# Running the fp32 transposes of a retention and mixture-of-adapters kernel as pairs of 64-row array tiles

## The chip, the cores and the metric

The kernel runs on one core of one Trainium2 chip. TensorE (PE) multiplies, and its weight loads are shown as an engine of their own (PEld); VectorE (DVE) and ScalarE (ACT) read what it leaves in PSUM; GpSimd (POOL) works on SBUF alone; SyncE (SP) issues transfers. The metric is the device time of one execution in microseconds (us); lower is better. A difference under 1% can't be told from no change here.

## The reference

```python
# q, k, v: [8 batches, 8 heads, 576 rows, 64]
scores = scale * q @ k.transpose(0, 1, 3, 2)
gamma  = 1.0 - 2.0 ** (-5.0 - arange(H))
ret    = scores * where(rel >= 0, gamma ** rel, 0.0)     # rel = row - column: causal decay
x      = (ret @ v) as [4608 tokens, 512]                 # heads side by side
# mixture of adapters: 8 experts of rank 16, the best 2 of each token
logits = x @ w_gate
w      = softmax over the 2 largest logits
out    = x + sum over those two of w * (x @ A[e]) @ B[e]
```

## The kernel before

The rows are cut into chunks of 128 (four full ones, and a last one of 64). A **unit** is one chunk of a pair of batches: 16 full units (t = 0 to 15, chunk by chunk, four batch pairs in each) and 4 half units (t = 16 to 19). Two units in a row share one load: a **quad**, which is q, k and v of four batches for one chunk. A quad is loaded by one transfer each for q, k and v (the first quad by halves), and up to three quads are in SBUF (`io`, 3 buffers). `issue(n)` names the quad two ahead of the one in work.

For each unit the code writes these stages, and each engine does its own in the order that a scheduling layer made of the code, close to the written one:

- **T** (`stage_T`, L191): q and k, which lie with rows on partitions, are transposed on TensorE (L206) to `pt_q` and `pt_k` in PSUM: 16 transposes of 128x128 fp32 in a full unit, 8 in a half one. DVE multiplies `pt_q` by the decay `aqp` into `qT` (L219), ACT copies `pt_k` into `kT` (L228).
- **S** (`stage_S`, L234): scores of two heads at once, on two 64-row halves of the array (L261), then the causal mask on DVE into `rt` (L272; `rh` in half units, L280).
- **O** (`stage_O`, L293): the carried state `P` times `qT` into `px` (L309; not in the first chunk), and the new state `pu` from k and v (L323), added on DVE (`pn`) and decayed on POOL. v has been scaled before on POOL (`scale_v`, L184).
- **R** (`stage_R`, L345): `rt` times v onto `px` (L358; L376 in half units). ACT copies `px` to `xT`, which is x transposed.
- **Z** (`stage_Z`, L389): x times all A and the gate, into `pz` (L396); then a chain of small operations that picks two experts: DVE `lg`, `m8`, `ns`, ACT `sg` (L417), DVE `cm`, `zc`.
- **X** (`stage_X`, L436): `zc` is transposed (fp16, L442) and copied to `zT` by ACT.
- **Y** (`stage_Y`, L450): `xT` is transposed back into `po` (L457, 4 transposes of 128x128 fp32 for each batch, 8 in a full unit), the adapter output is added there (L466, fp16), ACT copies `po` to `osb`, and SP writes it out.

A full unit is written S(t), O(t), R(t), X(t-1), T(t+1), Y(t-1), Z(t). PSUM has 8 buffers of one bank each (`pp`), which all these tiles share in turn. The constants `pack` (identities, masks, decays), `aqp`, A and the gate are loaded from ACT's queue at the start, beside the first q and k on SP's.

Of the kernel before, what the change touches and what calls it, by code (L numbers as in the profile page):

```python
# [18 lines left out]
def kernel(  # L19
# [10 lines left out]
    nc = tc.nc  # L30
# [17 lines left out]
    swap_np = np.roll(np.eye(128, dtype=np.float32), 64, axis=1)  # L48
# [6 lines left out]
    for hp in range(HP):  # L55
# [25 lines left out]
    swap32 = pack[:, 128:256]
    tri = pack[:, 256:384]
    trih = pack[:, 384:448]
    gv = pack[:, 448 : 448 + H]
    gvh = pack[:, 448 + H : 448 + 2 * H]
    g128 = pack[:, 448 + 2 * H : 448 + 2 * H + HP]
# [52 lines left out]
    aqp = cpool.tile([128, HP, 128], FP32, tag="aqp", name="aqp")  # L139
    nc.scalar.dma_start(out=aqp, in_=dr_aqp.ap())  # L140
    AW = []
    for par in range(2):
        AW.append(cpool.tile([128, HP, ER + E], FP32, tag=f"AW{par}", name=f"AW{par}"))
    for dt in range(HP):
        nc.scalar.dma_start(
            out=AW[0][:, dt, 0:ER].rearrange("p (e r) -> p e r", e=E),
            in_=moe_A[:, 128 * dt : 128 * dt + 128, :].rearrange("e d r -> d e r"),
        )
        nc.scalar.dma_start(
            out=AW[0][:, dt, ER : ER + E],  # L150
            in_=moe_w_gate[128 * dt : 128 * dt + 128, :],
        )
    Bcat = cpool.tile([128, Dm], FP16, tag="Bcat", name="Bcat")
    nc.gpsimd.dma_start(out=Bcat, in_=moe_B.rearrange("e r d -> (e r) d"))
    ident16 = cpool.tile([128, 128], FP16, tag="ident16", name="ident16")
    nc.gpsimd.tensor_copy(out=ident16, in_=ident32)
    for ho in range(2):
        nc.gpsimd.tensor_copy(
            out=AW[1][64 * ho : 64 * ho + 64],
            in_=AW[0][64 - 64 * ho : 128 - 64 * ho],  # L160
        )
    issue(1)

# [8 lines left out]
    ]  # L172

# [17 lines left out]
    def stage_T(t):  # L191
# [5 lines left out]
        nb = 2 if full else 1  # L197
        hpg = 2 if full else 4
        L = 128 if full else LH
        for g in range(HP // hpg):  # L200
            for src, dst, nm in ((q32, qT, "q"), (k32, kT, "k")):
                ps = pp.tile([128, hpg, nb, 128], FP32, tag="pb", name=f"pt_{nm}")
                for a in range(hpg):
                    hp = g * hpg + a
                    for b in range(nb):
# [8 lines left out]
                pv = ps.rearrange("p a b (c i) -> p a (b c) i", i=L)  # L214
                dv = dst.rearrange("p a b i -> p a (b i)")[
                    :, g * hpg : g * hpg + hpg, 0 : 2 * L
                ].rearrange("p a (b i) -> p a b i", i=L)
                if nm == "q":
                    nc.vector.tensor_tensor(  # L219
                        out=dv,  # L220
                        in0=pv,
                        in1=aqp[:, g * hpg : g * hpg + hpg, 0:L]
                        .unsqueeze(2)
                        .broadcast_to((128, hpg, 2, L)),
                        op=ALU.mult,
                    )
                else:
                    nc.scalar.copy(out=dv, in_=pv)  # L228
# [64 lines left out]
    def stage_O(t):  # L293
# [10 lines left out]
        if c > 0:  # L304
# [40 lines left out]
    def stage_R(t):  # L345
# [24 lines left out]
        else:  # L370
            for hp in range(HP):
                for b in range(2):
                    for ho in range(2):
# [6 lines left out]
                            start=False,  # L380
# [3 lines left out]
            xt = mo.tile([128, HP, 128], FP32, tag="xT", name="xT", bufs=6)  # L384
            for b in range(2):
                nc.scalar.copy(out=xt[:, :, LH * b : LH * b + LH], in_=px[b])  # L386
# [62 lines left out]

    def stage_Y(t):  # L450
# [3 lines left out]
        for b in range(len(s["xT"])):  # L454
            po = pp.tile([128, Dm], FP32, tag="pb", name="po")
            for dt in range(HP):
                nc.tensor.matmul(  # L457
                    po[:, 128 * dt : 128 * dt + 128],
                    lhsT=s["xT"][b][:, dt, :],
                    rhs=swap32 if b else ident32,  # L460
                    is_transpose=True,
                    start=(dt == 0),
                    stop=False,
                    skip_group_check=True,
                )
            nc.tensor.matmul(  # L466
                po, lhsT=s["zT"][:, b, :], rhs=Bcat, start=False, stop=True,
                skip_group_check=True,
            )
            osb = mo.tile([128, Dm], FP32, tag="osb", name="osb", bufs=4)  # L470
            nc.scalar.copy(out=osb, in_=po)  # L471
            if full:
                n0 = S * (2 * bp + b) + 128 * c
                nc.sync.dma_start(out=out[n0 : n0 + 128, :], in_=osb)
            else:
                for par in range(2):
                    n0 = S * (2 * bp + par) + 128 * c
# [6 lines left out]
    scale_v(0)  # L484
    for t in range(NU):
# [18 lines left out]
        stage_Z(t)  # L504
# [33 lines left out]
```

## Time and profile before

| | |
|---|---|
| median of 3 runs | 226.03 us (224.5 to 226.05) |
| the profiled execution | 225.21 us |
| its span in the profile | 223.4 us |
| busy: TensorE, its weight loads | 200.8 us (90%), 182.4 us (82%) |
| busy: DVE, ACT, POOL | 105.9 us (47%), 80.6 us (36%), 59.8 us (27%) |
| moved by DMA | 39.11 MB, 175 GB/s over the span |

The profiled execution is 0.4% under the median. What lies outside its span is 1.8 us.

### The profile page before, as it was taken

To read this page: it belongs to the slowest core of one execution; us is meant where nothing else is said; L and a number is where in the kernel's file an instruction comes from. 1 tells how busy PE (TensorE), PEld (TensorE's weight loads), DVE (VectorE), ACT (ScalarE), POOL (GpSimd) and SP (SyncE) were. 2 spreads that over 40 slices of the span, in tenths; PEclk is the share of its full clock that TensorE was granted. 3 is DMA by queue.
4 is the path that set the end of the run, shared out by engine and by line. 5 is a ranking of instruction groups with operands and counts; after the bars stand their busy time and mean duration, and the time that the engine had idled before them with its cause. 6 is when DMAs were issued, how large, how long until landed. Compare 5 with 4: busy or idle time off the path is not lost.

```text
span 223.4 us, 7090 instructions
## 1 busy us (share of the span) xinstructions
PE 200.8 (90%) x3096; PEld 182.4 (82%) x3096; DVE 105.9 (47%) x272; ACT 80.6 (36%) x170; POOL 59.8 (27%) x61
## 2 busy tenths in 40 slices
PE   0197979899999899999999999999999999999951
PEld 0186969698999799999999989999999999978840
DVE  0115552827273927272727292727272727244430
ACT  0041525051513260616161506161615151544431
POOL 3016320711812520902530622090501321000000
PEclk9999999999999999999999999999999999999995
DMA  7999998999699999999999798967555520222212
GB/s 167 182 201 220 189 230 185 218 221 234 141 230 271 211 204 237 271 201 213 303 222 191 227 203 194 220 191 183 139 130 147 140 89 7 98 97 50 50 47 47
DMA packets 57342, 39.11 MB, mean 175 GB/s; under 512 B 30816, under 2 KB 52576, under 8 KB 57312
## 3 DMA queue, kind: packets, MB, share of 16 engines
q1 hardware_dynamic: 52144, 37.75, 75.0%
q10 hardware_dynamic: 5024, 0.78, 2.7%
q8 instruction: 24, 0.39, 0.8%
q0 software_dynamic: 144, 0.13, 0.4%
q14 instruction: 6, 0.05, 0.1%
HBM read 29.35 MB, written 9.44 MB: 174 GB/s over the span
## 4 chain that ended last, share of the span: by engine, by line
PE 73%; DMA 9%; DVE 8%; SPq 5%; ACT 1%; issue 1%; ACTq 1%
PE pz L396 14%; PE px L358 11%; PE ps_s L261 10%; PE po L457 7%; PE px L309 6%; PE pt_k L206 6%; PE pt_q L206 6%; DMA k<-in_k_dram 6%; PE pu L323 5%; SPq L98 5%; PE po L466 4%; DMA AW<-in_moe_A_dram 3%; DVE rt L272 3%; DVE cm L422 2%; PE pzt L442 2%
## 5 line engine op out<-in xcount | busy, mean ns | idle before, releaser
L219 DVE TENSOR_TENSOR qT<-pt_q,aqp 128x512 f32<-128x512 f32 x36 | 24.9, 692 | 48.9 <-PE pt_q L206 48.9
L184 POOL TENSOR_TENSOR v<-v,pack 128x512 f32<-128x512 f32 x36 | 36.6, 1042 | 35.1 <-DMA v<-in_v_dram 34.8
L367 ACT COPY xT<-px 128x512 f32<-128x512 f32 x32 | 18.8, 587 | 69.6 <-PE px L358 69.6
L338 POOL TENSOR_TENSOR P<-pn,gdec 128x512 f32<-128x512 f32 x16 | 20.4, 1276 | 81.4 <-DVE pn L337 62.3
L272 DVE TENSOR_TENSOR rt<-ps_s,pack 128x512 f32<-128x512 f32 x64 | 39.6, 682 | 2.2 <-PE ps_s L261 2.2
L396 PE MATMUL pz<-AW,xT 128*128 128x136 f32 x288 | 36.7, 279 | 0.7 <-ACT xT L386 0.7
L396 PEld LDWEIGHTS pz<-AW,xT 128*128 128x128 f32 x288 | 35.9, 190 | 1.4 <-ACT xT L386 0.9
L261 PE MATMUL ps_s<-qT,kT 64*128 64x128 f32 (+1 forms) x640 | 36.7, 272 | 0.0
L261 PEld LDWEIGHTS ps_s<-qT,kT 64*128 64x128 f32 (+1 forms) x640 | 33.1, 181 | 2.8 <-issue 0.3
L358 PE MATMUL px<-rt,v 128*64 128x128 f32 x512 | 34.4, 275 | 0.8 <-DVE rt L272 0.7
L358 PEld LDWEIGHTS px<-rt,v 128*64 128x64 f32 x512 | 29.1, 137 | 3.0 <-DVE rt L272 2.5
L206 PE MATMUL pt_q<-pack,q 128*128 128x128 f32 x144 | 22.9, 283 | 7.2 <-DMA q<-in_q_dram 7.2
L409 DVE COPY lg<-pz 128x16 f32<-128x16 f32 (+1 forms) x20 | 3.5, 173 | 50.1 <-PE pz L396 50.1
L206 PE MATMUL pt_k<-pack,k 128*128 128x128 f32 x144 | 22.6, 281 | 4.4 <-DMA k<-in_k_dram 4.4
L228 ACT COPY kT<-pt_k 128x512 f32<-128x512 f32 x36 | 21.2, 588 | 12.0 <-PE pt_k L206 12.0
L471 ACT COPY osb<-po 128x512 f32<-128x512 f32 x36 | 21.0, 586 | 5.1 <-PE po L466 2.8
L206 PEld LDWEIGHTS pt_q<-pack,q 128*128 128x128 f32 x144 | 16.6, 145 | 7.5 <-issue 7.3
L417 ACT ACTIVATE sg<-lg,ns 128x8 f32<-128x8 f32 x36 | 9.1, 294 | 36.1 <-DVE ns L412 36.1
L457 PE MATMUL po<-pack,xT 128*128 128x128 f32 x144 | 21.9, 274 | 0.0
L206 PEld LDWEIGHTS pt_k<-pack,k 128*128 128x128 f32 x144 | 17.5, 145 | 5.0 <-DMA k<-in_k_dram 3.7
L323 PE MATMUL pu<-v,k 128*64 128x64 f32 x512 | 18.9, 225 | 1.7 <-POOL v L184 1.7
L323 PEld LDWEIGHTS pu<-v,k 128*64 128x64 f32 x512 | 16.4, 138 | 4.7 <-POOL v L184 2.3
(28 smaller groups left out, 137.5 us busy)
## 6 DMA issues: line engine op xcount, KB each, us to landing
out_dram<-osb SPq DMA_DIRECT2D x32, 256.0 KB, 3.7
q<-in_q_dram SPq DMA_DIRECT2D x2, 512.0 KB, 7.2
k<-in_k_dram SPq DMA_DIRECT2D x2, 512.0 KB, 9.0
v<-in_v_dram SPq DMA_DIRECT2D x2, 512.0 KB, 7.1
q<-in_q_dram SPq DMA_DIRECT2D x8, 128.0 KB, 3.8
k<-in_k_dram SPq DMA_DIRECT2D x8, 128.0 KB, 3.2
v<-in_v_dram SPq DMA_DIRECT2D x8, 128.0 KB, 3.5
out_dram<-osb SPq DMA_DIRECT2D x8, 128.0 KB, 2.3
```

Source lines behind the costliest of these rows:

```text
L184: nc.gpsimd.tensor_tensor(out=v32[:, b * H : b * H + H, :], in0=v32[:, b * H : b * H + H, :], in1=g.unsqueeze(2).broadcast_to((128, H, Dh) ...
L206: nc.tensor.matmul(ps[:, a, b, :], lhsT=src[:, b * H + 2 * hp : b * H + 2 * hp + 2, :], rhs=ident32, is_transpose=True, start=True, stop=True,
L219: nc.vector.tensor_tensor(out=dv, in0=pv, in1=aqp[:, g * hpg : g * hpg + hpg, 0:L] .unsqueeze(2) .broadcast_to((128, hpg, 2, L)), op=ALU.mult,
L228: nc.scalar.copy(out=dv, in_=pv)
L261: nc.tensor.matmul(o, lhsT=kT[sl, hp, b, :], rhs=qT[sl, hp, b, :], start=(a == 0 and (b == 0 or not full)), stop=True, skip_group_check=True,)
L272: nc.vector.tensor_tensor(out=r.rearrange("p a b i -> p (a b) i"), in0=ps[ho].rearrange("p a b i -> p (a b) i"), in1=tri.unsqueeze(1).broa ...
L323: nc.tensor.matmul(pu[64 * ho : 64 * ho + 64, hp, b, :], lhsT=s["k"][:, b * H + h, :], rhs=s["v"][:, b * H + h, :], start=(hp == 0 and b = ...
L338: nc.gpsimd.tensor_tensor(out=pf, in0=pn, in1=gdec.rearrange("p a b d -> p (a b d)"), op=ALU.mult,)
L358: nc.tensor.matmul(px[b][64 * cc : 64 * cc + 64, hp, :], lhsT=s["v"][:, b * H + h, :], rhs=rt[h][:, b, :], start=(c == 0 and hp == 0), sto ...
L396: nc.tensor.matmul(pz[:, b, :], lhsT=xts[b][:, dt, :], rhs=AW[b][:, dt, :], start=(dt == 0), stop=(dt == HP - 1), skip_group_check=True,)
L457: nc.tensor.matmul(po[:, 128 * dt : 128 * dt + 128], lhsT=s["xT"][b][:, dt, :], rhs=swap32 if b else ident32, is_transpose=True, start=(dt ...
L471: nc.scalar.copy(out=osb, in_=po)
```

## The change

Every 128x128 fp32 transpose becomes two products: rows 0 to 63 and rows 64 to 127 of the source are each loaded as weights (64 rows, 128 columns) and meet a 64x64 identity (`id64`), so that each gives 64 output columns. The two go to two PSUM banks. `stage_T` makes two tiles for q and two for k, by row half and no longer by head pair; the fp32 transposes of Y stand in a stage of their own, `stage_B`; `stage_Y` keeps the fp16 products, now four of 256 columns in place of two of 512, and four copies of 256 elements in place of two of 512. A unit is now written S(t), O(t), R(t), T(t+1), B(t-1), X(t-1), Z(t), Y(t-1), for half units too. In half units the state's product goes to a bank of its own (`pq`), ACT copies it, and DVE adds `px` to it in place of ACT's copy. `osb` has 3 buffers for both batches in place of 4 for one. Constants are split and go through SP's queue: `id64` first, `aqp` behind the first q, `pack` behind the first k, A and the gate behind the first v. A `Sigmoid` on one element at the start makes ACT load its table there.

```diff
+    id64 = cpool.tile([128, 64], FP32, tag="id64", name="id64")
+    nc.sync.dma_start(out=id64, in_=dr_first.ap())
+    warm = cpool.tile([128, 1], FP32, tag="warm", name="warm")
+    nc.scalar.activation(out=warm, in_=warm, func=AFT.Sigmoid)
...
+                if split and lo == 0 and src is k:
+                    nc.sync.dma_start(out=aqp, in_=dr_aqp.ap())
+                if split and lo == 0 and src is v:
+                    nc.sync.dma_start(out=pack, in_=dr_rest.ap())
+                if split and lo == 2 and src is q:
+                    load_moe()
...
-                        nc.tensor.matmul(
-                            ps[:, a, b, :],
-                            lhsT=src[:, b * H + 2 * hp : b * H + 2 * hp + 2, :],
-                            rhs=ident32,
...
+            for hp in range(HP):
+                for b in range(2 if full else 1):
+                    for r in range(2):
+                        sl = slice(64 * r, 64 * r + 64)
                         nc.tensor.matmul(
+                            ps[r][:, hp, b, :] if full else ps[r][:, hp, :],
+                            lhsT=src[sl, b * H + 2 * hp : b * H + 2 * hp + 2, :],
+                            rhs=id64[sl, :],
                             is_transpose=True,
...
-            for b in range(2):
-                nc.scalar.copy(out=xt[:, :, LH * b : LH * b + LH], in_=px[b])
+            xt = s["xh"]
+            for b in range(2):
+                xs = xt[:, :, LH * b : LH * b + LH]
+                nc.vector.tensor_tensor(out=xs, in0=px[b], in1=xs, op=ALU.add)
...
+    def stage_B(t):
...
+        for b in range(n):
+            for dt in range(HP):
+                for cc in range(2):
+                    sl = slice(64 * cc, 64 * cc + 64)
+                    nc.tensor.matmul(
+                        po[cc][:, b, dt, :],
+                        lhsT=s["xT"][b][sl, dt, :],
+                        rhs=id64[sl, :],
+                        is_transpose=True,
...
     def stage_Y(t):
...
+        for cc in range(2):
+            for b in range(n):
                 nc.tensor.matmul(
+                    po[cc][:, b, :, :],
+                    lhsT=s["zT"][:, b, :],
+                    rhs=bv[:, :, cc ^ b, :],
...
+        for cc in range(2):
+            for b in range(n):
+                nc.scalar.copy(out=osb[:, b, :, cc ^ b, :], in_=po[cc][:, b])
...
-        full = units[t][0] < NFULL
-        if full:
-            stage_R(t)
-        if t > 0:
-            stage_X(t - 1)
-        if not full:
-            stage_Y(t - 1)
-            stage_R(t)
+        stage_R(t)
         if t + 1 < NU:
             stage_T(t + 1)
-        if full and t > 0:
+        if t > 0:
+            stage_B(t - 1)
+            stage_X(t - 1)
+        stage_Z(t)
+        if t > 0:
             stage_Y(t - 1)
-        stage_Z(t)
```

On TensorE, from the end of R to the next unit's scores, a full unit reads so before (a number behind a name is that of a buffer; weight loads of fp32 products are not listed apart):

```order
L442 MATMUL pzt<-ident_95,zc 128x128
L206 MATMUL pt_q<-pack,q_712 128x128 x4
L206 MATMUL pt_k<-pack,k_713 128x128 x4
...
L457 MATMUL po<-pack,xT 128x128 x4
L466 LDWEIGHTS zT
L466 MATMUL po<-Bcat,zT 128x512
...
L396 MATMUL pz<-AW_83,xT 128x136 x4
L396 MATMUL pz<-AW_84,xT 128x136 x4
L261 MATMUL ps_s_1378<-qT,kT 128x128
```

And so in the changed kernel, at the same place:

```order
L229 MATMUL pt_q<-id_70,q_1211 128x64 x16
L229 MATMUL pt_k<-id_70,k_1212 128x64 x16
L512 MATMUL po_1920<-id_70,xT 128x64
L512 MATMUL po_1921<-id_70,xT 128x64
...
L493 MATMUL pzt<-ident_80,zc 128x128
...
L447 MATMUL pz<-AW_77,xT 128x136 x4
L447 MATMUL pz<-AW_78,xT 128x136 x4
L533 LDWEIGHTS zT
L533 MATMUL po_1920<-Bcat,zT 128x256
...
L533 MATMUL po_1921<-Bcat,zT 128x256
```

The transposes of T and B now stand together, the fp16 transpose `pzt` behind them, and the adapter products between Z and the scores.

On ACT, one full unit before, from the copies of R to the `sg` of Z:

```order
L367 COPY xT<-px_1240 128x512
L367 COPY xT<-px_1241 128x512
L447 COPY zT<-pzt 128x256
L228 COPY kT<-pt_k 128x512 x2
L471 COPY osb<-po 128x512 x2
L417 ACTIVATE sg<-lg,ns 128x8 x2
```

And in the changed kernel:

```order
L417 COPY xT<-px_1052 128x512
L417 COPY xT<-px_1053 128x512
L250 COPY kT<-pt_k 128x8x64 x2
L498 COPY zT<-pzt 128x256
L543 COPY osb<-po_1152 128x4x64 x2
L468 ACTIVATE sg<-lg,ns 128x8 x2
L543 COPY osb<-po_1153 128x4x64 x2
```

The `sg` of Z(t) still stands behind two copies of `osb`, but these now wait for products that come after Z(t), not before it.

## Rows read from the trace of the kernel before

**Rows 1.** The page, part 1: busy time, share and instructions of each engine.

```profile
PE 200.8 (90%) x3096; PEld 182.4 (82%) x3096; DVE 105.9 (47%) x272; ACT 80.6 (36%) x170; POOL 59.8 (27%) x61
```

**Rows 2.** TensorE's timeline, one full unit: start, us, instruction, tile, count.

```profile
112.34 0.61 PE L206 MATMUL pt_q<-pack,q 128*128 128x128 f32 x4
...
114.09 0.60 PE L457 MATMUL po<-pack,xT 128*128 128x128 f32 x4
114.53 0.38 PE L466 MATMUL po<-Bcat,zT 128*128 128x512 f16 x1
...
115.40 2.02 PE L396 MATMUL pz<-AW,xT 128*128 128x136 f32 x16
117.34 2.06 PE L261 MATMUL ps_s<-qT,kT 64*128 64x128 f32 x32
119.33 1.10 PE L309 MATMUL px<-qT,P 64*64 64x128 f32 x32
120.36 1.15 PE L323 MATMUL pu<-v,k 128*64 128x64 f32 x32
121.34 1.92 PE L358 MATMUL px<-rt,v 128*64 128x128 f32 x32
123.19 0.29 PE L442 MATMUL pzt<-ident,zc 128*128 128x128 f16 x2
123.32 0.61 PE L206 MATMUL pt_q<-pack,q 128*128 128x128 f32 x4
```

**Rows 3.** Weight loads by line and form: count, busy us, mean ns of one, idle before.

```profile
L396 PEld LDWEIGHTS pz<-AW,xT 128*128 128x128 f32 x288 | 35.9, 190 | 1.4 <-ACT xT L386 0.9
...
L206 PEld LDWEIGHTS pt_k<-pack,k 128*128 128x128 f32 x144 | 17.5, 145 | 5.0 <-DMA k<-in_k_dram 3.7 <-issue 1.3
...
L323 PEld LDWEIGHTS pu<-v,k 128*64 128x64 f32 x512 | 16.4, 138 | 4.7 <-POOL v L184 2.3 <-issue 2.1
```

**Rows 4.** DVE's timeline in the same unit as Rows 2.

```profile
117.45 0.17 DVE L409 COPY lg<-pz 128x16 f32<-128x16 f32 x1 [2.90 <-PE pz L396]
...
119.19 2.48 DVE L272 TENSOR_TENSOR rt<-ps_s,pack 128x512 f32<-128x512 f32 x4
```

**Rows 5.** ACT's timeline in the same unit.

```profile
118.13 0.49 ACT L417 ACTIVATE sg<-lg,ns 128x8 f32<-128x8 f32 x2 [1.90 <-DVE ns L412]
```

**Rows 6.** ACT's copies by line and form.

```profile
L386 ACT COPY xT<-px 128x256 f32<-128x256 f32 x8 | 2.6, 375 | 0.0
```

**Rows 7.** TensorE's timeline, unit 2, the first of the second quad.

```profile
40.71 1.04 PE L323 MATMUL pu<-v,k 128*64 128x64 f32 x28 [0.61 <-POOL v L184]
41.83 1.54 PE L358 MATMUL px<-rt,v 128*64 128x128 f32 x10
43.53 1.52 PE L358 MATMUL px<-rt,v 128*64 128x128 f32 x22 [0.17 <-DVE rt L272]
...
48.17 2.02 PE L396 MATMUL pz<-AW,xT 128*128 128x136 f32 x16
```

**Rows 8.** POOL's timeline: v scaled as the second and the seventh quad land.

```profile
38.62 4.04 POOL L184 TENSOR_TENSOR v<-v,pack 128x512 f32<-128x512 f32 x4 [6.77 <-DMA v<-in_v_dram]
...
125.75 4.04 POOL L184 TENSOR_TENSOR v<-v,pack 128x512 f32<-128x512 f32 x4 [2.08 <-DMA v<-in_v_dram]
```

**Rows 9.** DVE's timeline in unit 2: `cm` beside POOL's work.

```profile
38.91 1.78 DVE L422 SCALAR_TENSOR_TENSOR cm<-lg,m,sg 128x8 f32<-128x8 f32 x2 [0.37 <-ACT sg L417]
```

**Rows 10.** Busy us (instructions) of PE, PEld, DVE, ACT, POOL; PE clock, DMA share, GB/s.

```profile
86.00:108.00 22.00, 22.00 (x350) 20.56 (x348) 11.68 (x31) 8.57 (x18) 6.55 (x6) 1.00 1.00 240
```

**Rows 11.** TensorE's timeline: Z of units 16 and 17, and R of unit 18.

```profile
199.43 1.09 PE L396 MATMUL pz<-AW,xT 128*128 128x136 f32 x8
...
204.56 1.09 PE L396 MATMUL pz<-AW,xT 128*128 128x136 f32 x8
...
208.14 0.69 PE L376 MATMUL px<-rh,v 64*64 64x64 f32 x32
```

**Rows 12.** DVE's timeline in unit 18: the masks before R.

```profile
207.10 0.74 DVE L280 TENSOR_TENSOR rh<-ps_s,pack 128x256 f32<-128x256 f32 x2
```

More of the change, by code (lines that the diff above doesn't have):

```diff
@@ L76, with load_moe @@
     pp = ctx.enter_context(tc.tile_pool(name="pp", bufs=8, space=bass.MemoryType.PSUM))
+    id64 = cpool.tile([128, 64], FP32, tag="id64", name="id64")
+    nc.sync.dma_start(out=id64, in_=dr_first.ap())
+    warm = cpool.tile([128, 1], FP32, tag="warm", name="warm")
+    nc.vector.memset(warm, 0.0)
+    nc.scalar.activation(out=warm, in_=warm, func=AFT.Sigmoid)
     pack = cpool.tile([128, NPK], FP32, tag="pack", name="pack")
-    nc.scalar.dma_start(out=pack, in_=dr_pack.ap())
+    aqp = cpool.tile([128, HP, 128], FP32, tag="aqp", name="aqp")
     ident32 = pack[:, 0:128]
[L81 to L86, printed above, removed]
+    tri = pack[:, 128:256]
+    trih = pack[:, 256:320]
+    gv = pack[:, 320 : 320 + H]
+    gvh = pack[:, 320 + H : 320 + 2 * H]
+    g128 = pack[:, 320 + 2 * H : 320 + 2 * H + HP]
+    AW = []
+    for par in range(2):
+        AW.append(cpool.tile([128, HP, ER + E], FP32, tag=f"AW{par}", name=f"AW{par}"))
+    Bcat = cpool.tile([128, Dm], FP16, tag="Bcat", name="Bcat")
+    ident16 = cpool.tile([128, 128], FP16, tag="ident16", name="ident16")
+    def load_moe():
+        for dt in range(HP):
+            nc.sync.dma_start(
+                out=AW[0][:, dt, 0:ER].rearrange("p (e r) -> p e r", e=E),
+                in_=moe_A[:, 128 * dt : 128 * dt + 128, :].rearrange("e d r -> d e r"),
+            )
+        nc.sync.dma_start(
+            out=AW[0][:, :, ER : ER + E],
+            in_=moe_w_gate.rearrange("(t p) e -> p t e", p=128),
+        )
+        nc.gpsimd.dma_start(out=Bcat, in_=moe_B.rearrange("e r d -> (e r) d"))
     nat = {}
@@ L137 @@
     issue(0)
[L139 to L161, printed above, removed]
     issue(1)
+    nc.vector.tensor_copy(out=ident16, in_=ident32)
     gdec = cpool.tile([128, HP, 2, Dh], FP32, tag="gdec", name="gdec")
@@ L172, with swap_aw @@
     ]
+    def swap_aw():
+        for ho in range(2):
+            nc.gpsimd.tensor_copy(
+                out=AW[1][64 * ho : 64 * ho + 64],
+                in_=AW[0][64 - 64 * ho : 128 - 64 * ho],
+            )
     units = [(c, 2 * qd + s) for c, qd in quads for s in range(2)]
@@ L213, in stage_T @@
                         )
[L214 to L226, printed above, removed]
-                else:
-                    nc.scalar.copy(out=dv, in_=pv)
+            for r in range(2):
+                if full:
+                    o = dv[:, :, :, 64 * r : 64 * r + 64]
+                    if nm == "q":
+                        nc.vector.tensor_tensor(
+                            out=o,
+                            in0=ps[r],
+                            in1=aqp[:, :, 64 * r : 64 * r + 64]
+                            .unsqueeze(2)
+                            .broadcast_to((128, HP, 2, 64)),
+                            op=ALU.mult,
+                        )
+                    else:
+                        nc.scalar.copy(out=o, in_=ps[r])
+                else:
+                    o = dv[:, :, r, :]
+                    if nm == "q":
+                        nc.vector.tensor_tensor(
+                            out=o, in0=ps[r], in1=aqp[:, :, 0:64], op=ALU.mult
+                        )
+                    else:
+                        nc.scalar.copy(out=o, in_=ps[r])
         view = lambda tl: tl.rearrange("p a b i -> p a (b i)")[:, :, 0 : 2 * L].rearrange(
@@ L303, in stage_O @@
         s["px"] = px
-        if c > 0:
+        if not full:
+            pq = pp.tile([128, HP, 2, LH], FP32, tag="pb", name="pq")
+            for hp in range(HP):
+                for b in range(2):
+                    for ho in range(2):
+                        sl = slice(64 * ho, 64 * ho + 64)
+                        nc.tensor.matmul(
+                            pq[sl, hp, b, :],
+                            lhsT=P[bp][sl, hp, b, :],
+                            rhs=qT[sl, hp, b, :],
+                            start=(hp == 0 and b == 0),
+                            stop=True,
+                            skip_group_check=True,
+                        )
+            xt = mo.tile([128, HP, 128], FP32, tag="xT", name="xT", bufs=6)
+            nc.scalar.copy(
+                out=xt.rearrange("p a (b i) -> p a b i", i=LH), in_=pq
+            )
+            s["xh"] = xt
+        elif c > 0:
             for hp in range(HP):
@@ L448, in stage_X @@
         s["zT"] = zt
+    def stage_B(t):
+        s = st[t]
+        n = len(s["xT"])
+        po = [
+            pp.tile([128, n, HP, 64], FP32, tag="pb", name=f"po{cc}") for cc in range(2)
+        ]
+        for b in range(n):
+            for dt in range(HP):
+                for cc in range(2):
+                    sl = slice(64 * cc, 64 * cc + 64)
+                    nc.tensor.matmul(
+                        po[cc][:, b, dt, :],
+                        lhsT=s["xT"][b][sl, dt, :],
+                        rhs=id64[sl, :],
+                        is_transpose=True,
+                        start=(dt == 0 and b == 0),
+                        stop=False,
+                        skip_group_check=True,
+                    )
+        s["po"] = po
     def stage_Y(t):
```

66 lines of the change are left out of this document (35 added, 31 removed).

## The prediction

> **What bounds the kernel now.** I read the page's busy times first, then TensorE's timeline of one unit in the middle, then the weight loads by form, and last the waits of the units at the start and the end. TensorE is busy 200.8 of 223.4 us [rows 1], and in the middle it has no gap: a full unit takes from 112.34 to 123.32, 10.98 us, and each stage starts where the one before ends [rows 2]. In start to start times: T 1.75 for 16 transposes (109 ns each), a batch of Y 0.44 for four transposes and about 0.22 for its fp16 product, Z 1.94, S 1.99, px 1.03, pu 0.98, R 1.85. ACT (8.57 of 22 us) and POOL have room [rows 10]. DVE is idle half of the time but is nearly as late: its mask ends at 119.19 + 2.48 = 121.67, and R, which starts at 121.34, needs the last mask with its fifth product [rows 2, 4]. So what comes off TensorE between R and Z is gained in full, and what comes off between Z and R only as far as DVE's chain is not later. DMA is near full, with a share of 1.00 [rows 10].
>
> **The price of a pair.** A 128x128 transpose becomes two products of 64 columns with 64-row weights of 128 columns. No row shows this form as a transpose. By columns: 64 of the 128 that take 109 ns, so 55 ns if the halves run side by side. By likeness: `pu` is also two products at a time with 64 moving columns, two loads and two outputs for each pair; 16 pairs take 0.98, 61 ns [rows 2]. From above: S has 64-row weights of 128 columns and pairs them, but moves 128 columns; 16 pairs in 1.99 are 124 ns [rows 2], no less than one transpose now. The two ends differ in what paces a pair, the moving columns or the weights. The loads decide for me: fp32 weights of 128 columns take 190 ns in Z and of 64 columns 138 in `pu`, but in a transpose 128 columns take 145 [rows 3], as short as half the weights. I take 61 ns; the ends are 55 and 124.
>
> [...]
>
> **T and B.** A full unit has 16 + 8 transposes on the path: 24 x 109 = 2.62 us now, 24 x 61 = 1.46 then: -1.16.
>
> **The order of stages.** S, the one stage that follows products of the full array with products of half rows, takes 124 ns a pair and R with equally many columns 116 [rows 2]: 16 x 8 ns = 0.13 us, which I read as the price of changing the shape. Before, R is followed by X and Z by S; now R by T, B by X, Y by S: one change more, +0.13 (0 to 0.26). Net -1.03 for a full unit.
>
> **Y behind Z.** Four fp16 products of 256 columns move what two of 512 did: 0 (to +0.1 if the two extra loads of `zT` show). They now stand between Z and S, 0.44 us, and so give DVE's chain that much more time before R; but `sg` stands behind the two copies of the first `po`. If the end of Z's issue is 0, those copies start at about 0.3 (two products of 0.11 and their tail), take 0.375 each by the half copies [rows 6], overlapping a little, and end near 1.05, where `sg` started at 118.13 - 117.34 = 0.79 before [rows 2, 5]. The chain is 0.3 later and R 0.44 + 0.1 later: DVE is covered with 0.2 us to spare. If that cover is gone, up to 0.4 us comes back in each unit. The second `po` is free at about 1.05 + 0.5 (`sg`) + 0.7 = 2.3; should the next `px` share its bank, it begins at 0.44 + 2.1 = 2.5. Also covered, barely. ACT's four short copies take what the two long ones did.
>
> **The start.** Unit 2 can't begin earlier than its v: it lands at 38.62, POOL scales two parts of four by 40.7, and 28 of the 32 `pu` products wait until 40.71 [rows 7, 8]. Splitting and moving constants changes what lands first, not the bytes that go ahead of this v, so I leave 38.62 where it is (1.5 us either way), and earlier first transposes, the earlier table load and the moved copies are worth nothing: all lie ahead of this wait. R begins at 41.83 as before, but stalled until 43.53 for DVE, whose `cm` took 1.78 beside POOL's scaling [rows 7, 9]. In the changed kernel Y no longer stands ahead of Z(1), so this chain should be through before POOL starts: R ends at 43.7, T and B take 24 x 61 = 1.46, with 0.12 for X, and Z(2) starts at 45.3 in place of 48.17: -2.85 (from -1.3, if the stall stays, to -3.3).
>
> **The middle.** From Z(2) to Z(14) are 12 full units: 12 x -1.03 = -12.4. Loads don't hold them: between the second quad's v and the seventh's, at 38.62 and 125.75, lie 17.4 us for each quad [rows 8], and two units will need 2 x 9.95 = 19.9.
>
> **The end.** From Z(14) to Z(16), 16 pairs lie in each unit: 2 x (16 x -0.048 + 0.13) = -1.3. The other half units took 204.56 - 199.43 = 5.13 [rows 11]. There the chain decides: the masks end at 207.84, 3.28 after Z(17) began [rows 11, 12]; add 0.3 for `sg` behind the copies, 0.65 for R, and 0.85 for two new DVE adds, which are as large as the masks (0.37 each) and only partly beside T and B: 5.1. Nothing gained there, 0 to +0.4 for each of three. The last Z to the end: 0.
>
> **Sum.** -2.85 - 12.4 - 1.3 = -16.6, from the profiled execution's 225.21: 208.6. The median lies 0.4% above that execution, so I say **208.5 us**.
>
> **Rivals.**
> 1. *The weights pace a pair.* Two loads of 128 columns for 64 moved columns leave no time to hide the second. At S's 124 ns the 344 pairs on the path (24 at the start, 288, 32) cost 344 x 63 ns = 21.7 more: 230 us, slower than before. It decides above the price at which 344 pairs eat 16.6 us, 61 + 48 = 109 ns. For it: S is the only pair with such weights. Against it: rows 3. Between the two, at a transpose's own 109 (halves that don't run side by side would also give that, and the change would not do what it says), 225 us, no change. [...]
> 2. *The race behind Z is lost.* If `sg` behind the copies, or `px` behind the second `po`, costs 0.3 to 0.6 in each of 13 units, 4 to 8 come back: 212.5 to 216.5. A DVE operation caught beside POOL's scaling costs up to 1.36 a time [rows 9], and with the shorter unit more quads might catch it: four more are 5 us.
> 3. *The loads become the bound.* With a share of 1.00 [rows 10] a faster TensorE asks for more at once. If a quad then takes 21 us instead of 17.4, six of them cost 6 x 1.1 = 6.6: 215. Against it: in the trace the landings run ahead of their use, more with every quad.
>
> **How the numbers follow.** Forecast 0.70 (205 to 212); rival 2 0.12; rival 3 0.06; no change 0.05; slower by rival 1 0.07. The range 205 to 217 holds the first three, about 0.85, and leaves out rival 1 and no change; a pair at 55 ns (206.5) and both ends of the start lie in it. Faster by over 1% (about what a measurement of this kernel can tell) 0.88, same 0.05, slower 0.07.
>
> **What would show it.** T's 32 products in 0.9 to 1.0 us start to start, B's 16 in under 0.5, transposing loads no longer than 145 ns, a full unit of 9.8 to 10.0 us without a gap on TensorE. Wrong would be pairs at over 100 ns; gaps before R with DVE as the releaser, or before `px` with ACT; TensorE waiting for q, k or v after unit 2; Z(2) later than 47.

## The result, and the profile after

The changed kernel takes 207.69 us (median of 4 runs, 207.16 to 208.97); the kernel before took 225.88 us beside it (4 runs). The ratio is 0.9209, with a 95% interval of 0.9156 to 0.9262. The forecast of 208.5 us and its range held. The profiled execution took 207.16 us with a span of 205.1, where [rows 1] belong to a span of 223.4: 18.3 us less.

The page of the changed kernel, part 1, as in [rows 1]: busy time, share of the span and instructions of each engine.

```profile
PE 183.8 (90%) x3564; PEld 166.2 (81%) x3564; DVE 108.7 (53%) x286; ACT 76.6 (37%) x206; POOL 59.6 (29%) x60
```

TensorE lost 17.0 us of busy time and is still busy for 90% of the span: it still sets the end. Its timeline in a middle unit, to be held against [rows 2]: start, us, instruction, tile, count.

```profile
91.56 0.71 PE L229 MATMUL pt_q<-id,q 64*128 64x64 f32 x16
92.11 0.66 PE L229 MATMUL pt_k<-id,k 64*128 64x64 f32 x16
92.60 0.66 PE L512 MATMUL po<-id,xT 64*128 64x64 f32 x16
93.19 0.29 PE L493 MATMUL pzt<-ident,zc 128*128 128x128 f16 x2
93.31 2.07 PE L447 MATMUL pz<-AW,xT 128*128 128x136 f32 x16
95.22 0.60 PE L533 MATMUL po<-Bcat,zT 128*128 128x256 f16 x4
95.75 2.06 PE L291 MATMUL ps_s<-qT,kT 64*128 64x128 f32 x32
97.74 1.10 PE L359 MATMUL px<-qT,P 64*64 64x128 f32 x32
98.77 1.15 PE L373 MATMUL pu<-v,k 128*64 128x64 f32 x32
99.75 1.92 PE L408 MATMUL px<-rt,v 128*64 128x128 f32 x32
101.60 0.58 PE L229 MATMUL pt_q<-id,q 64*128 64x64 f32 x12
```

The unit goes from 91.56 to 101.60: 10.04 us in place of 10.98, without a gap. Start to start, T takes 1.04 (1.75 before) and B 0.59 for eight pairs. The 16 products of k, which stand between two others of their own kind, take 92.60 - 92.11 = 0.49 us: 61 ns for each of eight pairs. Z (1.91), S (1.99), `px` (1.03), `pu` (0.98) and R (1.85) take what they took.

Where the 18.3 us came from is read from the starts of Z, in [rows 7, 11] and here:

```profile
43.47 2.07 PE L447 MATMUL pz<-AW,xT 128*128 128x136 f32 x16
...
164.02 2.07 PE L447 MATMUL pz<-AW,xT 128*128 128x136 f32 x16
...
180.17 1.15 PE L447 MATMUL pz<-AW,xT 128*128 128x136 f32 x8
...
195.68 1.17 PE L447 MATMUL pz<-AW,xT 128*128 128x136 f32 x8 [0.40 <-ACT zT L498]
```

| stretch | before | after | difference | forecast |
|---|---|---|---|---|
| start to Z(2) | 48.17 | 43.47 | -4.70 | -2.85 |
| Z(2) to Z(14), 12 full units | 133.82 | 120.55 | -13.27 | -12.4 |
| Z(14) to Z(16) | 17.44 | 16.15 | -1.29 | -1.3 |
| Z(16) to Z(19) | 15.27 | 15.51 | +0.24 | 0 to +0.4 each |
| Z(19) to the end of the span | 8.7 | 9.42 | +0.72 | 0 |

The three terms in the middle came out near the forecast, the last is 0.72 us longer, and the first is far off. The way to it is plain in unit 2. The rows that answer to [rows 7 to 9], from POOL, DVE and TensorE:

```profile
34.34 4.04 POOL L197 TENSOR_TENSOR v<-v,pack 128x512 f32<-128x512 f32 x4 [4.62 <-DMA v<-in_v_dram]
...
34.35 1.04 DVE L463 SCALAR_TENSOR_TENSOR ns<-m 128x2 f32<-128x2 f32 x1
35.77 1.64 DVE L473 SCALAR_TENSOR_TENSOR cm<-lg,m,sg 128x8 f32<-128x8 f32 x2 [0.37 <-ACT sg L468]
...
38.55 1.54 PE L408 MATMUL px<-rt,v 128*64 128x128 f32 x10 [1.08 <-DVE rt L302]
40.25 1.52 PE L408 MATMUL px<-rt,v 128*64 128x128 f32 x22 [0.17 <-DVE rt L302]
```

The second quad's v lands at 34.34, not at the 38.62 that the forecast had pinned. And the DVE stall beside POOL's scaling, which the forecast let vanish, is still there: `ns` takes 1.04 and `cm` 1.64, and R waits 1.08 for the first mask. Two errors of opposite sign stand in one term, and the second hangs on the first: DVE's chain is through `cm` by 37.4 us, so it would have been clear of POOL's work if v had landed at 38.62.

### The profile page after: what moved, and what is told of

Same layout as the page of the kernel before. It is cut to its first block, busy times and chain, and to the rows that moved or that the text cites. A ratio compares the mean times of both kernels' runs of the same rounds, so it can differ in the third digit from the quotient of the medians.

```text
span 205.1 us, 8039 instructions
## 1 busy us (share of the span) xinstructions
PE 183.8 (90%) x3564; PEld 166.2 (81%) x3564; DVE 108.7 (53%) x286; ACT 76.6 (37%) x206; POOL 59.6 (29%) x60
## 4 chain that ended last, share of the span: by engine, by line
PE 72%; SPq 9%; DVE 7%; DMA 5%; ACT 3%; issue 1%; ACTq 0%
PE pz L447 16%; PE px L408 12%; PE ps_s L291 12%; PE pu L373 6%; PE px L359 6%; PE pt_q L229 5%; DMA k<-in_k_dram 5%; PE po L512 4%; SPq L127 4%; PE pt_k L229 4%; PE po L533 3%; DVE rt L302 2%; PE px L426 2%; ACT osb L543 2%; SPq L101 2%; PE pzt L493 2%
## 5 line engine op out<-in xcount | busy, mean ns | idle before, releaser
L291 PE MATMUL ps_s<-qT,kT 64*128 64x128 f32 (+1 forms) x640 | 37.4, 275 | 1.2 <-ACT kT L250 1.2
L241 DVE TENSOR_TENSOR qT<-pt_q,aqp 128x512 f32<-128x512 f32 x32 | 20.6, 686 | 31.1 <-PE pt_q L229 31.1
L447 PEld LDWEIGHTS pz<-AW,xT 128*128 128x128 f32 x288 | 34.7, 190 | 0.6 <-ACT zT L498 0.5
L543 ACT COPY osb<-po 128x256 f32<-128x256 f32 x72 | 23.1, 375 | 25.8 <-PE po L533 25.8
L250 ACT COPY kT<-pt_k 128x512 f32<-128x512 f32 x32 | 17.2, 589 | 19.2 <-PE pt_k L229 19.2
L229 PE MATMUL pt_q<-id,q 64*128 64x64 f32 x288 | 13.6, 234 | 6.7 <-DMA q<-in_q_dram 6.7
L229 PEld LDWEIGHTS pt_q<-id,q 64*128 64x128 f32 x288 | 10.8, 142 | 9.6 <-issue 9.4
L229 PE MATMUL pt_k<-id,k 64*128 64x64 f32 x288 | 12.8, 228 | 3.4 <-DMA k<-in_k_dram 3.4
L473 DVE SCALAR_TENSOR_TENSOR cm<-lg,m,sg 128x8 f32<-128x8 f32 x36 | 9.9, 294 | 8.8 <-ACT sg L468 8.8
L229 PEld LDWEIGHTS pt_k<-id,k 64*128 64x128 f32 x288 | 10.9, 143 | 3.8 <-issue 1.7
L359 PE MATMUL px<-qT,P 64*64 64x128 f32 x384 | 13.2, 275 | 0.0
```

The source lines that it names most:

```text
L229: nc.tensor.matmul(ps[r][:, hp, b, :] if full else ps[r][:, hp, :], lhsT=src[sl, b * H + 2 * hp : b * H + 2 * hp + 2, :], rhs=id64[sl, :], ...
L241: nc.vector.tensor_tensor(out=o, in0=ps[r], in1=aqp[:, :, 64 * r : 64 * r + 64] .unsqueeze(2) .broadcast_to((128, HP, 2, 64)), op=ALU.mult,)
L291: nc.tensor.matmul(o, lhsT=kT[sl, hp, b, :], rhs=qT[sl, hp, b, :], start=(a == 0 and (b == 0 or not full)), stop=True, skip_group_check=True,)
L359: nc.tensor.matmul(px[b][64 * cc : 64 * cc + 64, hp, :], lhsT=P[bp][64 * ho : 64 * ho + 64, hp, b, :], rhs=qT[64 * ho : 64 * ho + 64, hp, ...
L447: nc.tensor.matmul(pz[:, b, :], lhsT=xts[b][:, dt, :], rhs=AW[b][:, dt, :], start=(dt == 0), stop=(dt == HP - 1), skip_group_check=True,)
L543: nc.scalar.copy(out=osb[:, b, :, cc ^ b, :], in_=po[cc][:, b])
```

## Experiments

Ratios are to the kernel before, run on the same chip in the same job (medians 225.5 to 226.2 us).

**1. The changed kernel with whole transposes.** Order of stages, constants' queue and half units as in the changed kernel; T and B with 128x128 transposes, and with them Y's products and copies as wide as before (two of 512).

```diff
-   ps[r][:, hp, b, :], lhsT=src[sl, ...], rhs=id64[sl, :]      # 32 of 64 rows
+   ps[:, a, b, :],     lhsT=src[:, ...],  rhs=ident32          # 16 of 128 rows
```

> The changed order of stages, constants and half units, but every fp32 transpose in one product of the full array again, as before. Theory (the pairs are the gain: 61 ns in place of 109 for each of some 344 transposes on the path): 16.5 us come back, less about 1.3 for one change of array shape fewer in each unit, so 221 to 224 us. Rival (the new order of stages, Y behind Z above all, is a good part of the gain): 217 us or less.

Measured: 221.48 us (221.29 to 222.39), ratio 0.9827 (0.9776 to 0.9879). The pairs are worth 221.48 - 207.69 = 13.8 us. T and B of one unit, from the first line to the second, take 2.68 us here and 1.63 in the changed kernel:

```profile
107.28 0.66 PE L219 MATMUL pt_q<-id,q 128*128 128x128 f32 x4
...
109.96 0.28 PE L476 MATMUL pzt<-ident,zc 128*128 128x128 f16 x2
```

The whole unit takes 11.07 us, where the kernel before took 10.98: with whole transposes the new order costs 0.09 us a unit. What is left beside the pairs, about 4 us, is not what I took it for: see runs 5 and 9.

**2. The halves in turn.** The same products, but all those of the lower 64 rows of a tensor first, and then all those of the upper.

```diff
-  for hp in range(HP):
-      for b in range(2):
-          for r in range(2):
+  for r in range(2):
+      for hp in range(HP):
+          for b in range(2):
```

> The changed kernel, with all products of the upper row half of a tile ahead of those of the lower half, so that two products that follow each other use the same rows of the array. Theory (two halves run side by side, each paced by its 64 columns at about 55 ns): no product has a partner any more, T goes from 1.04 to about 1.8 us and B from 0.59 to about 0.95 in a full unit, 222 to 226 us. Rival (the halves are cheap one by one, or the weights pace them): within 2 us of 207.7.

Measured: 214.27 us (213.79 to 215.18), ratio 0.9499 (0.9454 to 0.9544): between the two. TensorE's timeline of this kernel shows why:

```profile
104.24 0.83 PE L229 MATMUL pt_q<-id,q 64*128 64x64 f32 x13
104.85 0.27 PE L229 MATMUL pt_k<-id,k 64*128 64x64 f32 x1
104.91 0.22 PE L229 MATMUL pt_q<-id,q 64*128 64x64 f32 x1
...
105.09 0.59 PE L229 MATMUL pt_k<-id,k 64*128 64x64 f32 x10
...
106.41 0.29 PE L493 MATMUL pzt<-ident,zc 128*128 128x128 f16 x2
```

In the program all 16 `pt_q` products stand ahead of the first `pt_k` one, yet a `pt_k` product for the other half of the rows starts between two of them. So the written order isn't kept between row halves, the halves overlap in part in this kernel as well, and T and B take 106.41 - 104.24 = 2.17 us, where the changed kernel takes 1.63 and one product after another, at the 0.06 us that lie between two starts on one row half here, would take 48 x 0.06 = 2.9. That the halves run side by side is borne out; that writing them apart would keep them apart was wrong, and with it the size that I expected (222 to 226 us). The rival, within 2 us of 207.7, falls too.

**6. Four quarters for q.** In full units q is transposed by four products of 32 rows and 32 columns in place of two of 64.

```diff
-  for r in range(2):
-      sl = slice(64 * r, 64 * r + 64)
+  for r in range(4):
+      sl = slice(32 * r, 32 * r + 32)
```

> The changed kernel with q transposed in full units by four 32-row products of 32 columns into four banks (k stays with pairs), four DVE products of 256 elements in place of two of 512. Theory (the moved columns pace a group): a group of four takes 30 to 40 ns and q's 32 products 0.3 us where k's 32 take 0.49; the time goes down by up to 3 us if the eight banks allow it. Rival (the 128-column weight loads pace it, at about 60 ns): a group takes 60 ns as a pair does, q's part of T stays at 0.5 us, and the time is 207 to 210.

Measured: 208.32 us (207.90 to 209.56), ratio 0.9217 (0.9182 to 0.9252), the changed kernel's own time. In its timeline of TensorE a group of four takes about what a pair does:

```profile
102.39 0.69 PE L232 MATMUL pt_q<-id,q 32*128 32x32 f32 x32
103.01 0.71 PE L232 MATMUL pt_k<-id,k 64*128 64x64 f32 x16
```

From start to start q's eight groups of four take 0.62 us, and k's eight pairs 103.56 - 103.01 = 0.55 (103.56 is the start of `po`). A group moves 32 columns where a pair moves 64, and takes no less: the columns don't pace a pair. Nor does the number of loads, which is four in a group and two in a pair.

**4. The stage order of before, with pairs.** R, X, T, B, Y, Z as the kernel before writes them.

```diff
         stage_R(t)
+        stage_X(t - 1)
         stage_T(t + 1)
         stage_B(t - 1)
-        stage_X(t - 1)
-        stage_Z(t)
         stage_Y(t - 1)
+        stage_Z(t)
```

> The changed kernel with the stages written in the order of before (R, X, T, B, Y, Z; in half units X, B, Y, R, T, Z). Theory (a change of array shape costs about 0.1 us, and Y behind Z gives DVE's chain 0.4 us): 0.2 to 0.35 us more for each full unit, 210 to 212.5 us, with R waiting for DVE's masks again. Rival (grouping by shape is most of the gain): 214 us or more.

Measured: 212.74 us (212.42 to 214.51), ratio 0.9443 (0.9389 to 0.9497). A steady unit takes 10.11 in place of 10.04, so the order is worth 0.07 us a unit, 1 us in all, where 0.2 to 0.35 was expected; this run doesn't separate the array's shape from Y's place behind Z. The rest of the 5 us is elsewhere: half units take 5.66 in place of 5.23, one middle unit takes 12.19 (Z at 126.24 and at 138.43) because `cm` is caught beside POOL's scaling, and unit 2 is caught there again. In unit 2 R waits 1.49 us for it, and then itself takes 4.5 us, at a granted clock of 0.50 for 2 us (columns of the second fence: stretch, its length, then busy us and count of PE, PEld, DVE, ACT, POOL, then granted clock, DMA share, GB/s):

```profile
38.54 4.53 PE L408 MATMUL px<-rt,v 128*64 128x128 f32 x32 [1.49 <-DVE rt L302]
```

```profile
40.00:42.00 2.00, 1.92 (x17) 1.76 (x17) 0.79 (x2) 0.58 (x1) 1.14 (x1) 0.50 0.88 237
```

**3. The constants on ACT's queue, as before.** Split as in the change, but issued by ACT, and the gate in four transfers as before.

```diff
-    nc.sync.dma_start(out=id64, in_=dr_first.ap())
+    nc.scalar.dma_start(out=id64, in_=dr_first.ap())   # pack, aqp, A and the gate too
```

> The changed kernel with its constants issued from ACT's queue beside the first q and k, as before. Theory (the order of the constants decides when the second quad's v lands, 34.3 us against 38.6, and unit 2 waits for it): v lands at 37.5 or later and the time is 209 to 212 us. Rival (the start is bound by the same bytes, and v landed earlier for another reason, such as less PE or ACT traffic): v lands at 34 to 35.5, time within 1 us of 207.7.

Measured: 205.69 us (205.21 to 206.93), ratio 0.9123 (0.9075 to 0.917). My theory falls, and the rival with it: this is 2.0 us faster than the change, all of it at the start (Z(2) at 41.39 in place of 43.47), and v lands 2.07 us earlier, at 32.27. SP's queue in the changed kernel, and then here:

```profile
7.69 4.37 SPq L101 DMA_DIRECT2D AW<-in_moe_A_dram  x4
12.11 1.12 SPq L105 DMA_DIRECT2D AW<-in_moe_w_gate_dram  x1
13.27 0.51 SPq L127 DMA_DIRECT2D q<-in_q_dram  x1
```

```profile
9.50 0.37 SPq L122 DMA_DIRECT2D v<-in_v_dram  x1
9.91 1.89 SPq L122 DMA_DIRECT2D q<-in_q_dram  x1
```

Issuing A and the gate keeps SP busy for 5.5 us, so that the second half of the first q is issued at 13.27 in place of 9.91. What the constants cost on that queue is the time to issue them.

**5. The kernel before once more,** unchanged, for the question why its v landed so late.

> The kernel before, unchanged, profiled once more. Its first profile shows 206 GB/s from 40 to 60 us and the second quad's v landing at 38.6 us; the changed kernel and all four experiments so far show 267 to 287 GB/s there and v at 32 to 34, the one with its constants loaded as before too. Theory (that execution's transfers were slow, and the kernel is not the cause): v lands at 32 to 35.5 and TensorE's middle is unchanged at 10.98 us a unit. Rival (something in the kernel before slows its transfers): v at 37.5 or later again.

Measured: one execution of 225.03 us; v landed at 38.48 again. So it is a property of the kernel. It isn't the whole transposes (run 1 has them and moves 268 GB/s between 20 and 60 us) nor ACT's queue (run 3 has it and moves 272). Left was something that no line of the diff shown says: where in SBUF the tiles lie. The kernel before starts the tiles for q, k and v at byte 36320 of a partition, the changed one at 36096, since its constants are 224 bytes shorter (an identity of 512 bytes has gone, `id64` with 256 and `warm` with 32 have come). The rows of q, k and v are 256 bytes long; 36096 is a multiple of 256, and 36320 is not.

**9, 10 and 11. Unused columns behind the constants,** so that all that lies behind them moves by 32 or 64 bytes, the tiles for q, k and v among it: in the kernel before (9) to a multiple of 256, in the changed kernel 32 (10) and 64 (11) past one. In 9 and 10 another pad keeps `osb` at its alignment to 64.

```diff
-    pack = cpool.tile([128, NPK], FP32, tag="pack", name="pack")
+    pack = cpool.tile([128, NPK + 8], FP32, tag="pack", name="pack")   # 11: + 16
```

> The kernel before with eight unused columns behind its constants, so that the tiles into which q, k and v are loaded start at byte 36352 of a partition, a multiple of 256, and no longer at 36320, which is 32 past a multiple of 64 (in the changed kernel they start at 36096, a multiple of 256). Nothing else moves but addresses. Theory: the address is what slows the transfers of the kernel before, 200 to 220 GB/s between 20 and 60 us against 250 to 280 in the others. Then they run at over 245 GB/s here, the second quad's v lands near 34 and not at 38.5, and the time is 221 to 223.5 us. Rival: it is something else in the kernel before (the order of its transfers, the constants ahead of them); then v lands at 38 to 39 and the time stays 225 to 226.5.

> The changed kernel with eight unused columns, 32 bytes, behind its constants: the tiles for q, k and v start 32 bytes past a multiple of 256, which is 32 past one of 64 as in the kernel before. Theory: transfers fall to 200 to 225 GB/s, the second quad's v lands 2.5 to 4.5 us later than 34.3, and the time rises by about as much, to 209.5 to 212.5 us. Rival, the address doesn't matter: 207.2 to 208.5.

> The changed kernel with 64 bytes of unused columns behind its constants: the tiles for q, k and v start at a multiple of 64 that is none of 256. If a packet of 256 bytes has to start at a multiple of 256, the transfers are as slow as with 32 bytes, and the time is 209.5 to 212.5; if a multiple of 64 is enough, they are as quick as in the changed kernel, and the time is 207 to 208.5.

Measured: run 9 takes 218.93 us (218.33 to 219.02), ratio 0.9681 (0.9645 to 0.9718): 7.2 us, more than I expected, from nothing but an address. Run 11 takes 213.56 us (212.66 to 215.64), ratio 0.9464 (0.9401 to 0.9528), which is also more than I expected. Run 10's four runs lie between 211.80 and 216.26 us, too wide for an interval, and nothing below rests on it. So a multiple of 64 is not enough (213.56 us, where the changed kernel took 207.69), and the change without its lucky address is worth 12.6 us, not 18. The stretch from 24 to 44 us (columns as above), first of the kernel before in run 5, then of run 9, then of run 11:

```profile
24.00:44.00 20.00, 17.76 (x238) 15.33 (x238) 11.31 (x28) 6.28 (x13) 5.70 (x6) 1.00 1.02 205
```

```profile
24.00:44.00 20.00, 18.87 (x252) 16.65 (x249) 12.10 (x26) 7.50 (x17) 6.59 (x6) 1.00 0.95 276
```

```profile
24.00:44.00 20.00, 18.03 (x296) 16.13 (x295) 10.14 (x28) 5.75 (x15) 8.40 (x8) 0.94 1.04 214
```

All three have the DMA engines near full (0.95 to 1.04), and move 205, 276 and 214 GB/s: the transfers themselves take longer. The queue that carries the loads and the outputs, in run 5 and then in run 9 (packets, MB, the time of its packets as a share of 16 engines' span):

```profile
q1 hardware_dynamic: 52144, 37.75, 76.2%
```

```profile
q1 hardware_dynamic: 52144, 37.75, 61.2%
```

A packet took 0.762 x 16 x 223.3 us / 52,144 = 52 ns in run 5, and 0.612 x 16 x 217.2 / 52,144 = 41 in run 9. The traces also keep each packet by its size, and there it is the loads that differ. Packets of 1,024 bytes, nearly all of them loads of whole quads, took 81 ns in the median in run 5 and 54 in run 9, 54 in the changed kernel and 76 in run 11. Packets of 2,048 bytes, nearly all of them outputs, took 84, 85, 84 and 84. The engines' own work doesn't mind the address: a full unit of run 9 takes 10.98 us as in [rows 2], and one of run 11 without a wait 10.05.

The side that moved for the loads is the one that is written, and there the packets took 54 ns against 81 and 76. On the side that is read the runs show no such difference: the output packets took 84 to 85 ns with `osb` 64, 96, 160 or 192 bytes past a multiple of 256 (runs 5, 8, 11, 9), and 84 with `osb` at one (run 12).

Where run 11 loses its time shows what a late landing costs beyond the start. POOL, DVE and TensorE in one of its middle units:

```profile
107.33 4.05 POOL L197 TENSOR_TENSOR v<-v,pack 128x512 f32<-128x512 f32 x4 [11.64 <-DMA v<-in_v_dram]
...
109.65 0.74 DVE L463 SCALAR_TENSOR_TENSOR ns<-m 128x2 f32<-128x2 f32 x1
110.76 1.86 DVE L473 SCALAR_TENSOR_TENSOR cm<-lg,m,sg 128x8 f32<-128x8 f32 x2 [0.37 <-ACT sg L468]
...
114.27 1.03 PE L408 MATMUL px<-rt,v 128*64 128x128 f32 x8 [0.17 <-DVE rt L302]
115.47 1.52 PE L408 MATMUL px<-rt,v 128*64 128x128 f32 x22 [0.17 <-DVE rt L302]
```

TensorE doesn't need this v yet. But POOL has waited for it and scales it at once, and DVE's `cm`, which takes 0.41 in a quiet unit, takes 1.86; this unit takes 11.62 us from Z (107.06) to Z (118.68).

**7. `ns` and `cm` with one tensor input in SBUF.** Each reads two; here `ns` takes the second as a scalar, and `cm` reads the logits from `pz` in PSUM in place of their copy.

```diff
-        nc.vector.scalar_tensor_tensor(out=ns, in0=m8[:, :, 0], scalar=-1.0, in1=m8[:, :, 1], ...)
+        for b in range(n):
+            nc.vector.tensor_scalar(out=ns[:, b : b + 1], in0=m8[:, b, 0:1], scalar1=-1.0,
+                                    scalar2=m8[:, b, 1:2], ...)
...
-                out=cm[:, b, :], in0=lg[:, b, :], ...
+                out=cm[:, b, :], in0=pz[:, b, ER : ER + E], ...
```

> The changed kernel with Z's two small DVE operations that read two tensors in SBUF made to read one: ns by tensor_scalar with the second value as a scalar operand, cm with the logits read from PSUM. Theory (an operation of DVE with two SBUF inputs waits while POOL's scaling runs; in unit 2 ns took 1.04 and cm 1.64 us in place of 0.16 and 0.42): no ns or cm over 0.5 us beside POOL, Z(2) 1.5 to 2.5 us earlier, 204.5 to 206.5 us. Rival (any small DVE operation waits there): the stalls stay and the time is within 1 us of 207.7.

Measured: 204.83 us (203.98 to 205.93), ratio 0.9071 (0.9029 to 0.9114). In unit 2, beside POOL's scaling from 33.42 to 37.47:

```profile
34.21 0.34 DVE L464 TENSOR_SCALAR ns<-m 128x1 f32<-128x1 f32 x2
34.90 0.41 DVE L474 SCALAR_TENSOR_TENSOR cm<-pz,m,sg 128x8 f32<-128x8 f32 x2 [0.35 <-ACT sg L469]
```

1.04 and 1.64 us have become 0.34 and 0.41. So the stall of these two went with their second tensor input in SBUF: beside POOL's scaling they take what they take in the next unit with POOL idle (0.33 and 0.41). Z(2) starts 2.1 us earlier, at 41.37; v also landed 0.9 us earlier in this execution, which the edit doesn't explain.

**8. Runs 3 and 7 together.** The two edits above.

> Both together: the changed kernel with the constants from ACT's queue as before, and ns and cm with one SBUF input. Theory (the two save different waits at the start): 205.7 less 1.5 to 2.5, 203 to 204.5 us, and below both kernels. Rival (the same wait seen from two sides, unit 2 waiting for its v): 205 to 206.

Measured: 203.85 us (203.08 to 204.44, 5 runs), ratio 0.9026 (0.8996 to 0.9056). The two savings, 2.0 and 2.9 alone, come to 3.8 together and not to 4.9: both lie mostly in the same start.

**12. Run 8 with the output tiles aligned.** `osb` starts at a multiple of 256 bytes in place of 32 past one of 64.

```diff
-        ns = mo.tile([128, n], FP32, tag="ns", name="ns")
+        ns = mo.tile([128, n + 8], FP32, tag="ns", name="ns")[:, 0:n]     # moves osb by 96 bytes
-            pn = wk.tile([128, HP * 2 * Dh], FP32, tag="pn", name="pn")
+            pn = wk.tile([128, HP * 2 * Dh + 8], ...)[:, 0 : HP * 2 * Dh]  # and by 64
```

> The version with constants from ACT's queue and DVE reading one SBUF tile at a time, and with osb, from which the output is written, moved to a multiple of 256 bytes (it started 32 past a multiple of 64). Theory, the address matters for transfers out of SBUF as well: the output lands in under 3.2 us where it took 3.7, and the last transfers end 0.2 to 0.7 us sooner: 203.0 to 203.6 us beside 203.85. Rival, only the side that is written matters, or the outputs are hidden: 203.6 to 204.1.

Measured: 202.94 us (202.47 to 203.32), ratio 0.898 (0.8951 to 0.901), the best of all. From the end of the last copy to the end of the span it takes 200.7 - 196.30 = 4.40 us, and 202.1 - 197.07 = 5.03 in run 8, as the theory had it. But the same stretch takes 4.44 in run 3 and 4.12 in run 7, which leave `osb` where it was, so 0.63 is no more than such executions differ by. The median landing of an output is 3.7 us here and 2.9 in run 8, against the theory, the output packets took 84 ns in both, and Z(2) is 1.1 us earlier, which the address of `osb` doesn't explain. The intervals of the two runs overlap: no effect of this edit is shown.

## Why the prediction was right, and where it was not

**The price of a pair: right, its reason in part.** 61 ns were forecast, and 61 measured where pairs follow pairs; over T and B with their changes of shape it is 1.63 / 24 = 68. So T (1.04), B (0.59) and the unit (10.04) came out just over the signs that the prediction had named (0.9 to 1.0, under 0.5, 9.8 to 10.0). The likeness to `pu` held in the number, with one thing to know: the trace counts a plain fp32 product twice (x32 for the 16 products of `pu`) and a transpose once (x16 for the 16 of k), so the 61 ns of `pu` were those of half a pair of products. Run 6 shows that the moved columns don't set the 61 ns. That the loads do is not shown; what sets it stays open. In the changed kernel, weight loads by line and form, as in [rows 3]:

```profile
L373 PEld LDWEIGHTS pu<-v,k 128*64 128x64 f32 x512 | 16.5, 137 | 2.7 <-issue 2.1 <-POOL v L197 0.2
L229 PEld LDWEIGHTS pt_k<-id,k 64*128 64x128 f32 x288 | 10.9, 143 | 3.8 <-issue 1.7 <-DMA k<-in_k_dram 1.5 <-PE pt_q L229 0.6
...
L512 PEld LDWEIGHTS po<-id,xT 64*128 64x128 f32 x288 | 10.5, 138 | 0.3 <-PE po L533 0.2
```

A transposing load of 128 columns takes 138 to 143 ns, what a plain one of 64 columns takes (137 in `pu`), where a plain one of 128 columns takes 190 in Z [rows 3]: here a load's time doesn't go by its columns alone. With 61 ns measured, rival 1 falls.

**The middle: the sum right, one part not foreseen.** A unit became 0.94 us shorter, not 1.03: T and B with their change of shape take 1.63, where 24 x 61 ns and 0.13 give 1.59, and Y's products take 0.53 behind Z, the 0.1 more that the forecast had left open. 12 x 0.94 is 11.3. The other 2.0 of the 13.27 are stalls of the kernel before that are gone, and run 9 shows which: with aligned tiles and nothing else, Z(2) to Z(13) takes 164.98 - 44.15 = 120.83, eleven units of 10.98, where the kernel before took 122.84.

**The race behind Z: won, as forecast.** `sg` stands behind two copies of `osb`, but DVE is through before R needs it. ACT, then DVE, in the next unit:

```profile
105.68 0.65 ACT L543 COPY osb<-po 128x256 f32<-128x256 f32 x2 [1.44 <-PE po L533]
106.22 0.50 ACT L468 ACTIVATE sg<-lg,ns 128x8 f32<-128x8 f32 x2
```

```profile
110.08 0.69 DVE L387 TENSOR_TENSOR pn<-pu,P 128x512 f32<-128x512 f32 x1 [0.32 <-PE pu L373]
```

DVE's last step of the unit now waits for TensorE; the masks before it end at 109.77, as R starts at 109.80. (R needs the last mask with its sixth product, not its fifth: in unit 2 it stops after x10 of x32, which are five products.)

**The step that failed is the start:** "Splitting and moving constants changes what lands first, not the bytes that go ahead of this v, so I leave 38.62 where it is". The bytes were the same, but not the time that they take: the constants' new size moved the tiles to a multiple of 256. Run 9 gives Z(2) at 44.15 for that alone, -4.02 of the term's -4.70. The rest of the term is a balance of things that I had put at nothing or at too much: pairs ahead of Z(2) gain, the constants on SP's queue cost 2.0 (run 3), and the DVE stall, "through before POOL starts" in the forecast, stayed, since POOL started earlier.

**So the sum was right partly by luck.** By medians, the way from one kernel to the other is: the address, -7.2 (run 9); order, half units and constants without pairs, +2.5 (from run 9 to run 1, which stand beside runs of the kernel before that differ by 0.7); the pairs, -13.8 (from run 1 to the change): -18.5, where -18.2 was measured. The forecast knew only the last of these well. At like addresses the change is worth 11.2 us (from run 9 to the changed kernel) or 12.6 (from the kernel before to run 11), where the forecast, which knew of no address, had 17.5 (from 226.03 to 208.5). Held against run 9, the stretches of the table above give -0.68, -11.27, -1.28, +0.23 and +0.90: of the -2.85 that the start was to bring, what the change writes brought 0.7.

Two steps of the sum were also off in themselves. The start's own figures (41.83 + 1.85 + 1.46 + 0.12 = 45.26) give -2.91, not -2.85. And a median 0.4% above 208.6 is 209.4, not 208.5; the measured 207.69 is 1.7 under that.

Had the tiles been 64 bytes off, the same code would have taken 213.6 us, inside the 212.5 to 216.5 of **rival 2**, and in part for the second of its reasons: DVE operations caught beside POOL's scaling, which make two of run 11's units 11.04 and 11.62 us long. Another 1.55 us are lost at the start, where Z(2) comes at 45.02. **Rival 3** would not have been true. In run 11 v lands every 17.3 us (from 38.45 to 142.54 in six quads), sooner than the 20.1 that two units take, and after unit 2 TensorE waits for no load. What the late landings do is to move POOL's scaling onto DVE's chain.

**The end** is 0.7 us longer than forecast. It lies behind the last copy (4.92 us, 3.94 in the kernel before), where the changed kernel and runs 3, 7, 8 and 12 take between 4.12 and 5.03; the cause stays open.

## What to carry to other kernels

When a diff changes the size of any tile, compute where the tiles behind it will start: here 32 bytes behind a table of constants were worth 7 us (run 9), more than a third of what the whole change brought. A fp32 transpose of 128x128 is worth writing as two 64-row products side by side (61 ns in place of 109 here, and 13.8 us in all by run 1), and no more than two (in run 6, 0.62 us for eight groups of four, 0.55 for eight pairs). And a small VectorE operation with two tensor inputs in SBUF in a critical chain is worth rewriting with one operand in PSUM or as a scalar, if GpSimd does long work beside it: in run 7, 1.04 and 1.64 us became 0.34 and 0.41, and the kernel took 2.9 us less.

## What the runs showed of the hardware that I had not expected

- Loads into SBUF ran faster into tiles that start at byte 36096 or 36352, both multiples of 256, than into tiles at 36320 or 36160; a tile 128 bytes past a multiple was not run. From 24 to 44 us all transfers together moved 276 GB/s with such tiles (run 9) and 205 to 214 with tiles 224 or 64 bytes past one (runs 5 and 11), with the DMA engines near full in each; a load's packet of 1,024 bytes took 54 ns in the median against 81 and 76.
- Products on the other half of the array's rows started ahead of their place in the program (run 2: `pt_k` at 104.85, `pt_q` still at 104.91).
- Four transposes on 32 rows each took about as long as two on 64 (run 6: 0.62 us for q's eight groups, 0.55 for k's eight pairs).
- In run 4, with R just released from a wait of 1.49 us, TensorE's granted clock fell to 0.50 for 2 us (40 to 42 us). In the changed kernel it stayed at 1.00 behind a wait of 1.08 us (at 38.55) and behind one of 1.57 (at 20.37). What decides isn't shown here.
